# First load ahead of the opening barrier, smaller last load, closing casts in separate tiles, and some loads in halves, in a decode layer on one core

## The chip, the cores and the metric

The kernel runs on one core of one Trainium2 chip. The metric is the device time of one execution in microseconds (us). Before and after are compared by runs of the same rounds on the same chip. A profile is one execution; its span runs from the first recorded instruction to the last, and is some 2 us shorter than the device time.

PE is TensorE's matmul side, PEld its weight loads, DVE is VectorE, ACT is ScalarE, POOL is GpSimd, SP is SyncE, which here issues nearly all transfers. "The stream" is the sequence of loads that SP's queue (q1) hands to the core's 16 DMA engines.

## The reference

One decode token for four sequences: layer norm, attention over the last 2,048 cached keys and values with 32 heads of 192, a gated feed-forward layer, and the sum of both with the input.

```python
B, Sq, D = 4, 1, 640;  Hq = Hkv = 32;  Sk = 8192;  Dh = 192;  F = 1536     # bf16
W = min(4096, max(256, Sk // 4))                  # 2048
q = (xn @ wq) ...                                 # xn = layernorm(x)
k, v = k_cache[:, :, Sk - W:, :], v_cache[:, :, Sk - W:, :]
o = softmax(q @ k.T * Dh ** -0.5) @ v             # per batch and head
return x + o.reshape(B, 1, Hq * Dh) @ wo + (silu(xn @ w1) * (xn @ w3)) @ w2
```

The K and V windows are nearly all of the data: 64 loads of 3 MB, against 22 MB for wq, wo, w1, w3 and w2.

## The kernel before

Every load is one transfer from SP's queue, in a fixed order. At the start come three pieces of wq and two K tiles; in the middle K, V, now and then wo, w1 and w3; at the end the last two V tiles, w2 in three pieces and the last two wo tiles. The opening barrier stands before all of it.

```python
x_sb = const.tile([B, D], BF16, name="x_sb")
nc.scalar.dma_start(out=x_sb[:], in_=A_x.rearrange("b s d -> (b s) d"))     # ACT's queue
for k0 in range(0, KC, 2):                                                  # wq, 3 pieces
    ...
    nc.sync.dma_start(out=wt[:, 0:n, :]..., in_=wq_v[:, k0:k0 + n, :]...)

def load_v(h):
    vt = vpool.tile([P, NJ, Dh], BF16, tag="vt")
    nc.sync.dma_start(out=vt[:].rearrange("q j d -> q (j d)"), in_=v_win[:, h]...)

def ffn_load(name, w):                                                      # w1, w3
    wt = fpool.tile([P, KC, F], BF16, tag="w", name=name)
    nc.sync.dma_start(out=wt[:]..., in_=w...)

W2C = [0, FC - 4, FC - 2, FC]            # FC = 12: pieces of 8, 2 and 2 chunks
def ffn_out(i):                          # two products (acc halves) for each chunk
    for c in range(*W2C[i:i + 2]):
        acc_add(hT[:, c, 0:B], ffn["w2"][:, c, :], last=(c == FC - 1))

# ... the last loads, in this order: V30, V31, w2 piece 0, wo, wo, w2 pieces 1 and 2

res = ppool.tile([NR, N0], BF16, tag="pr", name="res")                      # NR = 36, N0 = 320
nc.vector.tensor_copy(out=res[:, 0:N0 // 2], in_=acc[0:NR, 0:N0 // 2])
nc.scalar.copy(out=res[:, N0 // 2:N0], in_=acc[0:NR, N0 // 2:N0])
nc.sync.dma_start(out=out_v[:, 0:N0], in_=res[0:B, :])
nc.scalar.dma_start(out=out_v[:, N0:D], in_=res[CT:NR, :])
```

## Time and profile before

| | before |
|---|---|
| device time, median (3 runs) | 527.7 us (527.62 to 527.7) |
| span of the profile | 525.5 us |
| share of the 16 DMA engines' span that SP's queue took | 98.9% |
| PE / DVE / ACT busy | 67% / 66% / 9% |

The first view is the page of the kernel before: its first lines, and the lines of its DMA part (bytes moved, then for each queue the transfer packets, the MB and the share of 16 engines' span).

```profile
span 525.5 us, 4734 instructions
...
PE 354.6 (67%) x2307; PEld 74.0 (14%) x1613; DVE 345.2 (66%) x435; ACT 45.9 (9%) x144; POOL 1.1 (0%) x8
...
DMA packets 11572, 223.26 MB, mean 425 GB/s; under 512 B 1296, under 2 KB 1312, under 8 KB 2592
...
q1 hardware_dynamic: 11536, 222.97, 98.9%
q8 instruction: 15, 0.25, 0.2%
q14 instruction: 5, 0.04, 0.0%
```

No engine that computes is near full, and q1 fills the DMA engines. This is a kernel whose stream of loads is its time. Two things can still be read. The stream begins late and ends early in the span, and instructions are fetched over the same engines: q8 does it 15 times, 16 KB each, and q14 five times within the span, 8 KB each.

The next view is the timeline at both ends of the span: start, duration, engine, line, operation, output and inputs, count, and in brackets the idle time before it and what ended it.

```profile
0.73 1.35 SPq L131 DMA_DIRECT2D wt<-in_A_wq_dram  x3
0.74 0.56 ACTq L125 DMA_DIRECT2D x_sb<-in_A_x_dram  x1
...
2.74 0.47 DVE L160 CAST xf<-x_sb 4x640 f32<-4x640 bf16 x1
...
10.55 5.28 PE L193 MATMUL qps<-wt,xnT 128*128 128x512 bf16 x12 [2.20 <-DMA wt<-in_A_wq_dram]
...
521.12 0.44 PE L214 MATMUL acc<-w,hT 128*4 128x320 bf16 x4
521.83 0.44 PE L214 MATMUL acc<-w,hT 128*4 128x320 bf16 x4 [0.27 <-DMA w<-in_B_w_dram]
...
522.31 0.32 DVE L442 CAST res<-acc 36x160 bf16<-36x160 f32 x1 [2.63 <-PE acc L214]
522.66 0.28 ACT L443 CAST res<-acc 36x160 bf16<-36x160 f32 x1 [5.48 <-DVE res L442]
522.97 0.30 SPq L445 DMA_DIRECT2D out_dram<-res  x1
522.97 0.28 ACTq L446 DMA_DIRECT2D out_dram<-res  x1
```

The first load is issued 0.73 us into the span, behind the opening barrier, and its first packet starts at 1.77 us. At the end PE waits for the last piece of w2, four products take 0.44 us, and the two casts run one after the other: ACT's cast names DVE's as what it waited for, since both write one tile.

**Engine by engine.** The trace's packets can be chained to the engine that carried them, as on one engine each starts a few ns after the one before ended, and every engine carries the same sequence of packet sizes. This is a reading of the trace and no view of it; all 16 engines can be chained to their end. A "pause" is what a packet starts later than usual after the one before. The engines fall into two groups:

```
kernel before: end of the engine's last load (us), its instruction fetches, its pauses in all (us; over 60 ns each, after the first 9 us)
518.269  none           0           521.140  three of 8 KB   2.51
518.311  none           0           521.196  two of 16 KB    2.82
518.400  none           0           521.268  two of 16 KB    2.83
518.461  none           0           521.280  two of 16 KB    2.80
518.673  none           0           521.296  two of 16 KB    2.81
518.998  one of 8 KB    0.55        521.342  two of 16 KB    2.83
519.161  one of 8 KB    0.58        521.407  two of 16 KB    2.83
519.718  one of 16 KB   1.41        521.524  two of 16 KB    2.83
```

(Without the 0.08 and 0.11 us that two engines lose to the second x load.) Each 16 KB fetch of q8 costs its engine 1.41 us: the next packet starts some 0.9 us late, and the row after it takes some 0.5 us longer. The fetches of 8 KB cost 0.55 to 0.84 us. The q8 fetches go over eight of the engines in turn, so that with 15 of them seven engines have two and one has one. The Trainium skill describes these fetches ("Runtime: NRT & Kernel Launch", section "Instruction fetch mechanics"): instructions come in blocks of 16 KiB, 256 of them, by the sequencer's own DMA queue. The trace agrees in number: PE has 2,307 matmuls and 1,613 weight loads, 3,920 instructions, 15.3 blocks, and q8 shows 15 transfers. Whose instructions q14 fetches, no view shows.

### The profile page before, as it was taken

The page shows a single profiled execution, that of the slowest core. Times are in us where ns is not written, and L with a number is a line of the kernel's source. Part 1 is how long each engine was busy: PE and PEld are TensorE (multiplying, and loading weights), DVE is VectorE, ACT ScalarE, POOL GpSimd, SP SyncE. Part 2 cuts the span into 40 slices and gives each one's busy share as a digit, 9 for nine tenths or more (in the row PEclk, how much of TensorE's full clock was granted, in tenths as well). Part 3 has the DMA queues.
Part 4 walks back from the last instruction along what each step waited for, and adds up shares of the span by engine and source line. Part 5 has one row for each costly group of instructions (what it writes and reads, how often), then busy time and mean ns, then how long its engine had stood idle before and what let it go on. Part 6 is the DMA issues. An engine that isn't in the chain of part 4 may idle for free.

```text
span 525.5 us, 4734 instructions
## 1 busy us (share of the span) xinstructions
PE 354.6 (67%) x2307; PEld 74.0 (14%) x1613; DVE 345.2 (66%) x435; ACT 45.9 (9%) x144; POOL 1.1 (0%) x8
## 2 busy tenths in 40 slices
PE   2765766567747687667748866686685776675685
PEld 0000111111101111011111211111111111111122
DVE  3179755479557767587656776577667766677671
ACT  2111201000000001000000000000000000000001
POOL 0000000000000000000000000000000000000000
PEclk9989978979889979798887998789878998889988
DMA  8999999999999999999999999999999999999995
GB/s 360 430 438 425 440 431 424 436 428 439 425 433 431 435 426 432 434 427 439 430 427 440 425 434 430 436 428 435 432 428 434 430 430 436 430 434 430 434 422 240
DMA packets 11572, 223.26 MB, mean 425 GB/s; under 512 B 1296, under 2 KB 1312, under 8 KB 2592
## 3 DMA queue, kind: packets, MB, share of 16 engines
q1 hardware_dynamic: 11536, 222.97, 98.9%
q8 instruction: 15, 0.25, 0.2%
q14 instruction: 5, 0.04, 0.0%
q10 hardware_dynamic: 16, 0.01, 0.0%
HBM read 222.96 MB, written 0.01 MB: 424 GB/s over the span
## 4 chain that ended last, share of the span: by engine, by line
DMA 66%; PE 17%; DVE 14%; ACT 2%; issue 1%; SPq 0%
DMA kt<-in_A_k_cache_dram 52%; PE ps L244 10%; DVE pr L233 10%; DMA w<-in_B_w_dram 6%; DMA vt<-in_A_v_cache_dram 5%; PE po L317 4%; DMA wt<-in_A_wq_dram 4%; DVE sc L252 2%; PE qps L193 1%; ACT ex L280 1%; DVE z L288 1%; PE mt L274 1%; PE mt L261 0%; ACT negm L277 0%; DVE qbc L199 0%
## 5 line engine op out<-in xcount | busy, mean ns | idle before, releaser
L244 PE MATMUL ps<-pr,idb 128*128 128x512 bf16 x768 | 211.5, 417 | 151.0 <-DVE pr L233 151.0
L233 DVE TENSOR_TENSOR pr<-kt,qbc 128x3072 bf16<-128x3072 bf16 x128 | 223.5, 1747 | 113.8 <-DMA kt<-in_A_k_cache_dram 113.8
L252 DVE TENSOR_REDUCE sc<-ps 128x16 f32<-128x512 f32 x128 | 87.2, 681 | 2.1 <-PE ps L244 2.1
L296 PE MATMUL o_ps<-vt,z 128*8 128x384 bf16 x1024 | 57.4, 365 | 0.2 <-DVE z L288 0.2
L317 PE MATMUL po<-o_sb,sel_w 128*32 128x192 f32 x128 | 49.2, 518 | 0.6 <-ACT o_sb L299 0.6
L296 PEld LDWEIGHTS <-z 128*8 128x8 bf16 x1024 | 25.5, 92 | 91.7 <-issue 81.2
L299 ACT COPY o_sb<-o_ps 128x384 f32<-128x384 f32 x32 | 15.3, 478 | 190.1 <-PE o_ps L296 190.1
L288 DVE TENSOR_TENSOR z<-ex,mask_b 128x256 bf16<-128x256 bf16 x32 | 13.6, 424 | 23.4 <-ACT ex L280 23.4
L277 ACT COPY negm<-mt 128x1 f32<-128x1 f32 x32 | 5.1, 159 | 256.1 <-PE mt L274 256.1
L261 PEld LDWEIGHTS mt<-idf,lmax 128*1 128x1 f32 x32 | 3.2, 100 | 140.8 <-issue 140.8
L193 PE MATMUL qps<-wt,xnT 128*128 128x512 bf16 x60 | 16.1, 428 | 5.1 <-DMA wt<-in_A_wq_dram 5.1
L317 PEld LDWEIGHTS po<-o_sb,sel_w 128*32 128x32 f32 x128 | 13.8, 130 | 29.7 <-issue 28.2
L244 PEld LDWEIGHTS <-idb 128*128 128x128 bf16 x124 | 11.9, 96 | 39.1 <-issue 32.6
L274 PEld LDWEIGHTS mt<-ones_ff,gneg 1*128 1x128 f32 x64 | 9.4, 183 | 46.3 <-issue 20.9
L199 DVE CAST qbc<-qps 128x512 bf16<-128x512 f32 x6 | 3.8, 685 | 18.0 <-PE qps L193 18.0
L274 PE MATMUL mt<-ones_ff,gneg 1*128 1x1 f32 x64 | 12.1, 256 | 0.6 <-DVE gneg L269 0.6
L266 DVE TENSOR_REDUCE gmax<-mt 1x4 f32<-1x128 f32 x32 | 8.8, 274 | 5.4 <-PE mt L261 5.4
L304 PEld LDWEIGHTS po<-rsum,tot_w 128*32 128x32 f32 x64 | 4.4, 108 | 55.6 <-issue 30.6
L280 ACT ACTIVATE ex<-sc,negm 128x64 bf16<-128x64 f32 x32 | 11.1, 348 | 1.0
L261 PE MATMUL mt<-idf,lmax 128*1 128x128 f32 x32 | 11.0, 344 | 0.0
L214 PE MATMUL acc<-wo_t,oT 128*4 128x320 bf16 x96 | 9.2, 298 | 0.6 <-DMA wo_t<-in_A_wo_dram 0.6
L304 PE MATMUL po<-rsum,tot_w 128*32 128x1 f32 x64 | 7.1, 181 | 1.3 <-ACT ex L280 1.3
(53 smaller groups left out, 62.7 us busy)
## 6 DMA issues: line engine op xcount, KB each, us to landing
kt<-in_A_k_cache_dram SPq DMA_DIRECT2D x32, 3072.0 KB, 18.8
vt<-in_A_v_cache_dram SPq DMA_DIRECT2D x32, 3072.0 KB, 25.9
wo_t<-in_A_wo_dram SPq DMA_DIRECT2D x8, 960.0 KB, 21.5
wt<-in_A_wq_dram SPq DMA_DIRECT2D x2, 3072.0 KB, 9.8
w<-in_B_w_dram SPq DMA_DIRECT2D x2, 1920.0 KB, 21.5
wt<-in_A_wq_dram SPq DMA_DIRECT2D x1, 1536.0 KB
w<-in_B_w_dram SPq DMA_DIRECT2D x1, 1280.0 KB, 32.8
w<-in_B_w_dram SPq DMA_DIRECT2D x2, 320.0 KB, 31.0
```

What stands on the lines that cost most here:

```text
L193: nc.tensor.matmul(qp[:], lhsT=xnT[:, kc].rearrange("p a b -> p (a b)"), rhs=wq_rows[kc][:, (c0 + i) * QC:(c0 + i + 1) * QC], start=(kc == ...
L233: nc.vector.tensor_tensor(out=pr[:], in0=kts[h][:, g * JQ:(g + 1) * JQ, :], in1=qbc[:, h * Dh:(h + 1) * Dh].unsqueeze(1).to_broadcast([P, ...
L244: nc.tensor.matmul(ps[:], lhsT=idb[:], rhs=pr[:, :, kk * DD:(kk + 1) * DD], start=(kk == 0), stop=(kk == NK - 1))
L252: nc.vector.tensor_reduce(out=scs[h][:, g * JQ:(g + 1) * JQ], in_=pss.pop(u)[:], axis=AX.X, op=ALU.add)
L261: nc.tensor.transpose(out=mt[0:1, 0:P], in_=chs[h][0][:], identity=idf[:])
L274: nc.tensor.matmul(mt[:, P:P + 1], lhsT=gneg[:].rearrange("o p b -> o (p b)"), rhs=ones_ff[0:1, 0:1], start=True, stop=True)
L280: nc.scalar.activation(out=ex[:], in_=scs.pop(h)[:], func=ACTF.Exp, bias=negm[:, 0:1], scale=SCALE, accum_out=rsum[:])
L288: nc.vector.tensor_tensor(out=z[:], in0=ex[:].unsqueeze(2).to_broadcast([P, NJ, B]), in1=mask_b[:].unsqueeze(1).to_broadcast([P, NJ, B]), ...
L296: nc.tensor.matmul(o_ps[c * CT:c * CT + 2 * B, :], lhsT=z[:, 2 * jj:2 * jj + 2, :], rhs=vt[:, 2 * jj:2 * jj + 2, :], start=(jj < 4), stop= ...
L299: nc.scalar.copy(out=o_sb[:], in_=o_ps[:])
L304: nc.tensor.matmul(po[sl, Dh:Dh + 1], lhsT=tot_w[:].rearrange("p a b -> p (a b)"), rhs=rsums.pop(h)[:], start=True, stop=True)
L317: nc.tensor.matmul(po[sl, 0:Dh], lhsT=sel_w[:, par].rearrange("p a b -> p (a b)"), rhs=o_sb[:, par * Dh:(par + 1) * Dh].rearrange("p (r i) ...
```

## The change

Its intent is to start the stream earlier and to shorten what follows its end. The first wq transfer is moved into the block before the opening barrier. The last w2 piece shrinks from two chunks to one. The two closing casts write two tiles, each one half of the output, so that they can run together. w1, w3, the last two V tiles and the first eight chunks of w2 come in two transfers each. The second load of x is dropped (x_sb is used instead), and a tile of ones is cut to one element.

```diff
+def first_load_first(nc):
+    for f in nc.python_module().functions:
+        head, body = f.blocks[0], f.blocks[1]
+        ...                                   # i, ins: SP's first transfer in body
+        ...                                   # j: SP's drain, which opens the barrier, in head
+        del body.instructions[i]
+        head.instructions.insert(j, ins)
...
+    nc.at_finalize(first_load_first)
...
-    def load_v(h):
+    def load_v(h, n=1):
...
+        for j in range(0, NJ, NJ // n):
+            nc.sync.dma_start(out=vt[:, j:j + NJ // n]..., in_=...[:, :, j:j + NJ // n]...)
...
-    ones_ff = const.tile([P, P], FP32, name="ones_ff")
+    ones_ff = const.tile([1, 1], FP32, name="ones_ff")
...
-        nc.sync.dma_start(out=xr["t"][:], in_=A_x.rearrange("b s d -> (b s) d"))
...
-        nc.sync.dma_start(out=wt[:]..., in_=w...)                       # w1, w3
+        for k0, k1 in ((0, KC // 2), (KC // 2, KC)):
+            nc.sync.dma_start(out=wt[:, k0:k1, :]..., in_=...[:, k0:k1, :]...)
...
-    W2C = [0, FC - 4, FC - 2, FC]
+    W2C = [0, FC - 8, FC - 4, FC - 1, FC]
...
-        add(NU - 6, 0, load_v, h)
+        add(NU - 6, 0, load_v, h, 2)
     # last loads now: V30 (2), V31 (2), w2 pieces 0 and 1, wo, wo, w2 pieces 2 and 3
...
-    res = ppool.tile([NR, N0], BF16, tag="pr", name="res")
-    nc.vector.tensor_copy(out=res[:, 0:N0 // 2], in_=acc[0:NR, 0:N0 // 2])
-    nc.scalar.copy(out=res[:, N0 // 2:N0], in_=acc[0:NR, N0 // 2:N0])
+    res = [ppool.tile([NR, N0], BF16, tag="pr", name="res") for _ in range(2)]
+    nc.scalar.copy(out=res[1][CT:NR, :], in_=acc[CT:NR, :])
+    nc.vector.tensor_copy(out=res[0][0:B, :], in_=acc[0:B, :])
...
-    nc.sync.dma_start(out=out_v[:, 0:N0], in_=res[0:B, :])
-    nc.scalar.dma_start(out=out_v[:, N0:D], in_=res[CT:NR, :])
+    nc.scalar.dma_start(out=out_v[:, N0:D], in_=res[1][CT:NR, :])
+    nc.sync.dma_start(out=out_v[:, 0:N0], in_=res[0][0:B, :])
```

More of the change, by code (lines that the diff above doesn't have):

```diff
@@ L32, in keep_loaded_weights @@
                 del block.instructions[i]
+def first_load_first(nc):
+    for f in nc.python_module().functions:
+        head, body = f.blocks[0], f.blocks[1]
+        sp = mybir.EngineType.SP
+        i, ins = next((i, ins) for i, ins in enumerate(body.instructions)
+                      if ins.engine == sp and not isinstance(ins, mybir.InstNoOp))
+        assert isinstance(ins, mybir.InstDMACopy) and not ins.has_wait()
+        j = next(j for j, other in enumerate(head.instructions)
+                 if other.engine == sp and isinstance(other, mybir.InstDrain))
+        del body.instructions[i]
+        head.instructions.insert(j, ins)
 @with_exitstack
@@ L111, in load_k @@
         kts[h] = kt
-    def load_v(h):
+    def load_v(h, n=1):
         vt = vpool.tile([P, NJ, Dh], BF16, tag="vt")
-        nc.sync.dma_start(out=vt[:].rearrange("q j d -> q (j d)"),
-                          in_=v_win[:, h].rearrange("b (p j) d -> p b (j d)", p=PB))
+        for j in range(0, NJ, NJ // n):
+            nc.sync.dma_start(out=vt[:, j:j + NJ // n].rearrange("q j d -> q (j d)"),
+                              in_=v_win[:, h].rearrange("b (p j) d -> p b j d", p=PB)[:, :, j:j + NJ // n].rearrange("p b j d -> p b (j d)"))
         vts[h] = vt
@@ L220 @@
     po = ps_po.tile([P, Dh + 1], FP32, name="po")
-    xr = {}
-    def x_load():
-        xr["t"] = const.tile([B, D], BF16, name="x_res")
-        nc.sync.dma_start(out=xr["t"][:], in_=A_x.rearrange("b s d -> (b s) d"))
     def x_add(i):
-        acc_half(i, idb[0:B, 0:B], xr["t"], first=True)
+        acc_half(i, idb[0:B, 0:B], x_sb, first=True)
     def mult(u):
@@ L273, in chain_bc @@
         lmax, mt, gneg = chs[h]
-        nc.tensor.matmul(mt[:, P:P + 1], lhsT=gneg[:].rearrange("o p b -> o (p b)"), rhs=ones_ff[0:1, 0:1],
+        nc.tensor.matmul(mt[:, P:P + 1], lhsT=gneg[:].rearrange("o p b -> o (p b)"), rhs=ones_ff[:],
                          start=True, stop=True)
@@ L341, in ffn_load @@
         wt = fpool.tile([P, KC, F], BF16, tag="w", name=name)
-        nc.sync.dma_start(out=wt[:].rearrange("p k n -> p (k n)"), in_=w.rearrange("(p kc) n -> p (kc n)", kc=KC))
+        for k0, k1 in ((0, KC // 2), (KC // 2, KC)):
+            nc.sync.dma_start(out=wt[:, k0:k1, :].rearrange("p k n -> p (k n)"),
+                              in_=w.rearrange("(p kc) n -> p kc n", kc=KC)[:, k0:k1, :].rearrange("p k n -> p (k n)"))
         ffn[name] = wt
@@ L417 @@
     add(23, 9, ffn_h)
-    add(8, 0, x_load)
     add(16, 6, x_add, 0)
@@ L423 @@
     for h in range(H - 2, H):
-        add(NU - 6, 0, load_v, h)
+        add(NU - 6, 0, load_v, h, 2)
     add(NU - 6, 0, w2_load, 0)
+    add(NU - 6, 0, w2_load, 1)
     add(NU - 6, 0, wo_load, NG - 2)
     add(NU - 6, 0, wo_load, NG - 1)
-    add(NU - 6, 0, w2_load, 1)
     add(NU - 6, 0, w2_load, 2)
+    add(NU - 6, 0, w2_load, 3)
     add(e - 1, 8, ffn_out, 0)
+    add(e - 1, 8, ffn_out, 1)
     add(e - 1, 8, ge_proj, NG - 2, 0, RPP)
     add(e, 6, ge_proj, NG - 1, 0, RPP)
-    add(e, 7, ffn_out, 1)
     add(e, 7, ffn_out, 2)
+    add(e, 7, ffn_out, 3)
     for s in sorted(sched):
```

## The prediction

> **What bounds the kernel now.** The load stream. The DMA part of the page gives queue q1 98.9% of 16 engines' span, 222.97 MB at a mean of 425 GB/s; PE is busy 67% and DVE 66%.  Chaining the trace's DMA packets engine by engine, the undisturbed engines show no gap over 60 ns from the first packet at 1.8-2.5 us to their last at 518.3 us. Engines that also carried two 16 KB instruction fetches each (about 1.4 us apiece) end at 521.1-521.5 us. The last of them ends the kernel: the Trainium skill, "DMA: Bandwidth & Descriptors", section "Why a DMA increments its semaphore by 16 and not by 1", says that each engine posts its own increment after its data; the trace agrees (16 four-byte packets per full-width transfer). So only the stream's start, its engine time and what follows the last landing can move the time.
>
> **Terms**
>
> 1. *First wq transfer ahead of the barrier: -0.73 us.* In the timeline, SP reaches its drain at 0.00, is released at 0.65 and issues the first wq transfer at 0.73; POOL releases the barrier at 0.61. SP's issue takes 0.40 us, so it should still reach the barrier before POOL opens it. The next wq issue follows near 0.73 us; the first transfer lasts 7.3 us, so no hole appears.
> 2. *Five more transfers (w1, w3, two V, w2) over the same bytes: +0.2 us.* Completion packets of one engine are 7.272 us apart for 24,576-byte rows and 0.796 us for 2,560-byte rows (eight rows each): a fixed 0.043 us per transfer, times five. Dropping the second x load is worth under 0.02 us.
> 3. *Last w2 piece one chunk: -0.13 us.* In the timeline four products took 0.44 us after the last landing (521.83), a pair about 0.135 us. The three-chunk piece lands about 0.45 us before the last, so its six products are just issued when the last pair may start.
> 4. *Casts in separate tiles: -0.15 us.* Now DVE (0.32) and then ACT (0.28) run in series, 522.31 to the issue at 522.97: 0.66 us. After, both run together: DVE 320 columns, estimated from 0.317 us at 160 and 0.685 at 512, 0.48 us; ACT about 0.39. Then the issue.
> 5. *ones_ff smaller, the order of the w2 and wo loads, earlier w2 products:* off the critical path. The last loads get new waits on transfer semaphores, but over 10 us of loads are queued then.
>
> **Predicted time: 526.9 us** (527.7 - 0.8), range 526.2 to 527.6. Chances: faster by over 2% 0.003, within 2% 0.994, slower by over 2% 0.003.
>
> **What would show each step.** (1) The first wq issue at 0.00 of the new span, the first packet near 1.05 us and barrier release no later than 0.75. (2) Per-engine packets back to back, 0.043 us more per extra transfer; q1's share unchanged near 99%; PE's last wait still a w2 landing, near 521.3. (3) 0.30 us from last landing to end of products. (4) DVE and ACT casts overlapping, the longer one about 0.48 us. End of products to end of span: about 3.05 us (before 3.2).
>
> **What would make it wrong.** SP's drain may wait longer and hold the barrier. The x load now queues behind 24 KB packets, so xn comes up to 1 us later; if K tiles were then freed late enough to empty the queue, the stream would show a hole. Instruction fetches landing differently over the engines (three on one) would cost 1.4 us.

## The result

| | before | changed |
|---|---|---|
| device time, median (6 runs each) | 527.57 us (527.23 to 527.7) | 526.47 us (526.25 to 526.56) |
| span of the profile | 525.5 us | 524.4 us |
| ratio, 95% interval | | 0.998 (0.9967 to 0.9992) |

Ratios are the mean time of one kernel's runs over that of the other's of the same rounds, so not quite the ratio of the medians. The change is 1.1 us faster, 0.2%, well within 2%; the forecast was 526.9 us in a range of 526.2 to 527.6. It gained more than the 0.8 us that I had counted (by 0.3 us in the profiles, whose single terms can be compared), and the question is from where.

The same lines of the page, for the changed kernel:

```profile
span 524.4 us, 4738 instructions
...
PE 359.4 (69%) x2306; PEld 73.8 (14%) x1613; DVE 346.0 (66%) x435; ACT 46.0 (9%) x144; POOL 1.1 (0%) x8
...
DMA packets 12285, 223.26 MB, mean 426 GB/s; under 512 B 1373, under 2 KB 1513, under 8 KB 3177
...
q1 hardware_dynamic: 12248, 222.96, 99.2%
q8 instruction: 15, 0.25, 0.2%
q14 instruction: 6, 0.04, 0.0%
```

The bytes and the instruction fetches are the same (the sixth packet of q14 is one of 80 bytes at 0.09 us), and there are 712 more q1 packets. The timeline of the changed kernel at the two ends:

```profile
0.00 1.68 SPq L148 DMA_DIRECT2D wt<-in_A_wq_dram  x3
...
0.81 0.55 ACTq L142 DMA_DIRECT2D x_sb<-in_A_x_dram  x1
...
6.73 0.48 DVE L177 CAST xf<-x_sb 4x640 f32<-4x640 bf16 x1 [3.82 <-DMA x_sb<-in_A_x_dram]
...
12.94 16.05 PE L210 MATMUL qps<-wt,xnT 128*128 128x512 bf16 x59 [0.59 <-DVE xnT L201]
...
520.99 0.71 PE L231 MATMUL acc<-w,hT 128*4 128x320 bf16 x8 [0.15 <-DMA w<-in_B_w_dram]
...
521.73 0.48 DVE L457 CAST res<-acc 4x320 bf16<-4x320 f32 x1 [2.07 <-PE acc L231]
521.76 0.42 ACT L456 CAST res<-acc 4x320 bf16<-4x320 f32 x1 [4.59 <-PE acc L231]
522.21 0.28 ACTq L459 DMA_DIRECT2D out_dram<-res  x1
522.24 0.35 SPq L460 DMA_DIRECT2D out_dram<-res  x1
```

The first wq issue stands at 0.00. x is used 4 us later than before (6.73 against 2.74), as its small packets now queue behind rows of 24 KB; PE's first wq product starts at 12.94 instead of 10.55, but then runs through without a wait. At the end eight products run in one go, and the casts overlap.

To find the surplus I cut the whole execution at five moments that the trace gives, so that the phases add up to the span:

| phase (us) | before | changed | difference | forecast |
|---|---|---|---|---|
| span's start to first load packet | 1.765 | 1.039 | -0.73 | -0.73 |
| first packet to the end of the last load (the stream) | 519.759 | 520.036 | +0.28 | +0.2 |
| end of the last load to the end of the last product | 0.744 | 0.622 | -0.12 | -0.13 |
| last product to SP's output issue | 0.700 | 0.538 | -0.16 | -0.15 |
| SP's issue to its landing, as SP saw it | 1.473 | 1.374 | -0.10 | 0 |
| landing to the end of the span | 1.070 | 0.819 | -0.25 | 0 |
| sum | 525.511 | 524.428 | -1.08 | -0.8 |

Four terms are where they were forecast. The surplus lies after the output's issue, a stretch that I had taken as unchanged. There SP, as the last thing it does, goes through the semaphores of all transfers in a fixed order; the trace gives the time of each check:

```
SP's closing checks (semaphore numbers: start in us); * = semaphore of an output store
before    106*: 524.441   107,103*: 524.499   108,102: 524.566   109,100: 524.630   110,104: 524.692
changed   106,103: 522.644   107,102: 522.713   108,100: 522.779   109*,101: 523.430   110*,104: 523.609
```

Each check that follows the landing costs some 0.065 us. In the kernel before, the landing is waited for in the first check, and four more follow. In the changed kernel three checks are done while the stores are under way. This came about by counting: the transfers take eight semaphores in turn, and four transfers more (five halves, less one x load) move the two output stores from the first two checks to the last two.

### The profile page after: what moved, and what is told of

It is laid out like the page before. It is cut to its first block, busy times and chain, and to the rows that moved or that the text cites. A ratio compares the mean times of both kernels' runs of the same rounds, so it can differ in the third digit from the quotient of the medians.

```text
span 524.4 us, 4738 instructions
## 1 busy us (share of the span) xinstructions
PE 359.4 (69%) x2306; PEld 73.8 (14%) x1613; DVE 346.0 (66%) x435; ACT 46.0 (9%) x144; POOL 1.1 (0%) x8
## 4 chain that ended last, share of the span: by engine, by line
DMA 61%; DVE 21%; PE 15%; ACT 2%; issue 1%; SPq 0%
DMA kt<-in_A_k_cache_dram 52%; DVE pr L244 14%; PE ps L255 8%; DMA vt<-in_A_v_cache_dram 4%; DMA w<-in_B_w_dram 4%; DVE sc L263 3%; PE qps L210 3%; PE po L328 3%; DMA x_sb<-in_A_x_dram 1%; DVE z L299 1%; ACT ex L291 1%; PE mt L285 1%; ACT L291 0%; DVE oT L336 0%; DVE og L333 0%
## 5 line engine op out<-in xcount | busy, mean ns | idle before, releaser
L255 PE MATMUL ps<-pr,idb 128*128 128x512 bf16 x768 | 219.4, 429 | 146.2 <-DVE pr L244 146.1
L244 DVE TENSOR_TENSOR pr<-kt,qbc 128x3072 bf16<-128x3072 bf16 x128 | 223.4, 1746 | 108.5 <-DMA kt<-in_A_k_cache_dram 108.5
L307 PE MATMUL o_ps<-vt,z 128*8 128x384 bf16 x1024 | 54.4, 350 | 0.2 <-DVE z L299 0.2
```

The costliest lines, as they stand in the source:

```text
L244: nc.vector.tensor_tensor(out=pr[:], in0=kts[h][:, g * JQ:(g + 1) * JQ, :], in1=qbc[:, h * Dh:(h + 1) * Dh].unsqueeze(1).to_broadcast([P, ...
L255: nc.tensor.matmul(ps[:], lhsT=idb[:], rhs=pr[:, :, kk * DD:(kk + 1) * DD], start=(kk == 0), stop=(kk == NK - 1))
L307: nc.tensor.matmul(o_ps[c * CT:c * CT + 2 * B, :], lhsT=z[:, 2 * jj:2 * jj + 2, :], rhs=vt[:, 2 * jj:2 * jj + 2, :], start=(jj < 4), stop= ...
```

## The experiments

Theory A is the table of phases: the barrier, the last piece and the casts give what was forecast, extra transfers cost 0.04 to 0.05 us each, and a quarter of the gain is the accidental place of the output's semaphores. Rival B is the intent behind the change: that loads in halves, and the dropped x load, feed the queue better and gave the surplus.

All runs gave the right result. Unless said otherwise, "before" is the median of the kernel before in the same rounds.

| run | before | this | ratio (95%) | first packet | stream | load to product | product to issue | issue to landing | landing to end |
|---|---|---|---|---|---|---|---|---|---|
| a_barrier | 527.53 | 526.91 | 0.9986 (0.9973-1.0) | 1.030 | 519.805 | 0.747 | 0.701 | 1.474 | 1.069 |
| b_casts | 527.58 | 527.34 | 0.9995 (0.9982-1.0007) | 1.758 | 519.847 | 0.746 | 0.539 | 1.359 | 1.075 |
| c_w2 | 527.58 | 527.30 | 0.9998 (0.9984-1.0011) | 1.760 | 519.847 | 0.652 | 0.702 | 1.473 | 1.069 |
| d_lane_before | 527.58 | 527.30 | 0.9994 (0.9982-1.0007) | 1.761 | 519.847 | 0.746 | 0.702 | 1.479 | 0.812 |
| e_lane_after | 527.53 | 526.73 | 0.9983 (0.9971-0.9996) | 1.029 | 520.073 | 0.604 | 0.539 | 1.357 | 1.074 |
| f_whole | 527.53 | 526.46 | 0.9979 (0.9967-0.9992) | 1.027 | 520.080 | 0.643 | 0.538 | 1.381 | 1.047 |
| g_whole_lane | 527.53 | 526.32 | 0.9975 (0.9962-0.9987) | 1.023 | 519.842 | 0.643 | 0.539 | 1.366 | 0.813 |
| h_split24 | 527.58 | 527.65 | 1.0001 (0.9988-1.0013) | 1.033 | 521.207 | 0.653 | 0.539 | 1.368 | 0.812 |
| i_fetch | 527.49 | 527.77 | 1.0006 (0.9991-1.0021) | 1.026 | 521.345 | 0.721 | 0.540 | 1.371 | 0.813 |
| j_swap | 527.49 | 526.25 | 0.9977 (0.996-0.9993) | 1.028 | 519.868 | 0.636 | 0.473 | 1.229 | 0.997 |
| k_best | 527.63 | 526.19 | 0.9974 (0.996-0.9988) | 1.029 | 519.743 | 0.656 | 0.474 | 1.235 | 0.998 |

The intervals are some 0.13% wide to either side, 0.7 us, so for effects of 0.1 to 0.3 us the ratio decides nothing; the phases do, which repeat to about 0.01 us. (In f_whole SP was already waiting inside its first check when the store landed; there the end of that check is taken as the landing. In j_swap and k_best SP's store is the one checked first of the two, so their last two columns are to be compared by their sum alone.) Load to product is less steady (0.60 to 0.64 us with the same loads in the changed kernel, e_lane_after and j_swap). The stream is the exception: kernels with the same loads gave 519.76 to 519.85 us (before, a_barrier, b_casts, d_lane_before; c_w2, with its end pieces cut otherwise, 519.847) and 519.87 to 520.07 us (changed, e_lane_after, j_swap).

### a_barrier: the first load alone

```diff
# kernel before
+    nc.at_finalize(first_load_first)
```

> The kernel before with only the first wq transfer moved ahead of the opening barrier. Main theory (the stream of loads sets the time, so an earlier start shows in full): first load packet at 1.04 us instead of 1.77, everything after it as before, so 0.7 us faster than before (526.85 where before is 527.55). Rival (the late barrier and the x load, which arrives about 4 us later behind the queued packets, cost part of it): gain of 0.4 us or less, with holes between packets or a K tile freed late.

It ran 0.62 us faster than before. The first packet started at 1.030 us, 0.735 us earlier, and every later phase is that of the kernel before. In this run x came as late as in the changed kernel and the stream shows nothing of it (519.805 us), so the rival's loss is not there. The gain of an earlier start passes through to the end, 0.69 us of it in the span, the rest being within the scatter of the stream.

### b_casts and c_w2: the two ends of the tail alone

```diff
# b_casts, on the kernel before: only the lines of the closing casts and stores
# c_w2, on the kernel before
-    W2C = [0, FC - 4, FC - 2, FC]
+    W2C = [0, FC - 4, FC - 1, FC]
```

> The kernel before with only the two closing casts in separate tiles. Theory: end of the last product to SP's output issue 0.54 us instead of 0.70, so 0.16 us faster than before. Rival: none named beyond no gain (within 0.05 us), if the output's landing and not the issue sets the end.

> The kernel before with only the last w2 piece cut to one chunk (pieces of 8, 3 and 1 chunks, so no transfer more). Theory: last load's end to the end of the products 0.62 us instead of 0.74, so 0.12 us faster. Rival: no gain, as the three-chunk piece now holds PE up instead.

The casts alone cut the product-to-issue phase by 0.16 us as expected, and the issue-to-landing phase by 0.11 us as well, which I had not expected. The run was 0.24 us faster. The smaller last piece cut its phase by 0.09 us; the run was 0.28 us below before by its median, but its runs span 0.8 us and the mean differs by 0.02%, so its time is inconclusive and only the phase is shown.

The second part of the casts' gain is seen in every kernel with separate tiles, and in none without. In the former the two stores are issued by ACT and SP some 25 ns apart (110 ns in j_swap and k_best); in the kernels with one tile both wait for the same cast and are issued within 5 ns of each other. No run keeps one tile and moves the stores apart, so that the spacing is the cause is not shown.

### d_lane_before and e_lane_after: the place of the semaphores

Four loads of 32 bytes on ACT's queue in the middle of the kernel, whose data nobody uses, turn the count by four.

```diff
# d_lane_before on the kernel before, e_lane_after on the changed kernel
+    def tiny_load(i):
+        t = const.tile([1, 16], BF16, name=f"tiny{i}")
+        nc.scalar.dma_start(out=t[:], in_=A_x.rearrange("b s d -> (b s) d")[0:1, 0:16])
+    for i in range(4):
+        add(40 + 2 * i, 0, tiny_load, i)
```

> The kernel before with four 32-byte loads on ACT's queue in the middle, which turn the semaphores by four places: the output gets the two that SP checks last. Theory A: landing to end 0.82 us instead of 1.07, so 0.25 us faster than before though it does more work. Rival B: no change.

> The changed kernel with four 32-byte loads added in the middle on ACT's queue, which turn the eight transfer semaphores by four places, so that the output transfers get the ones that SP checks first at the end, as in the kernel before. Theory A (0.25 us of the measured 1.1 us came from this renumbering): SP does four more checks after the output has landed, landing to end 1.07 us instead of 0.82, so 0.25 us slower than the changed kernel (0.85 us faster than before). Rival B (the surplus over the forecast came from the finer loads or the dropped x load): nothing changes, 1.1 us faster than before.

With four useless loads the median of the kernel before fell by 0.28 us; its profile shows 0.26 us less in the last phase. With the same four the changed kernel lost: 0.80 us below before instead of 1.1, with 0.255 us more in the last phase. Rival B expected no change in either. The four lines below are from the view of one source line, the program's closing code, for the kernel before, the changed kernel, d_lane_before and e_lane_after in that order. They give SP's semaphore checks, their number, shortest, median and longest duration in ns, and the start of the first and the last in us.

```profile
L472 SPq EVENT_SEMAPHORE  x7: 17/28/28, 524.4 to 525.4; - x7
```

```profile
L486 SPq EVENT_SEMAPHORE  x7: 17/28/28, 522.6 to 524.4; - x7
```

```profile
L479 SPq EVENT_SEMAPHORE  x7: 17/28/28, 523.4 to 525.3; - x7
```

```profile
L493 SPq EVENT_SEMAPHORE  x7: 17/28/28, 523.6 to 524.6; - x7
```

(Seven records, as the two of the closing barrier are among them.) Where the stores' semaphores come last, the first check is done 1.7 to 1.9 us before the last record; where they come first, 1.0 us.

### f_whole and g_whole_lane: loads in one piece again

```diff
# f_whole, on the changed kernel
-        for k0, k1 in ((0, KC // 2), (KC // 2, KC)):
+        for k0, k1 in ((0, KC),):
...
-    W2C = [0, FC - 8, FC - 4, FC - 1, FC]
+    W2C = [0, FC - 4, FC - 1, FC]
...
-        add(NU - 6, 0, load_v, h, 2)
+        add(NU - 6, 0, load_v, h)
# g_whole_lane: the same, and five 32-byte loads as above, so that the count is as in the changed kernel
```

> The changed kernel with w1, w3, the last two V tiles and the front of w2 in one transfer each again (five fewer transfers; the last w2 piece stays one chunk). Theory A: the stream of loads is 0.2 us shorter (0.043 us per transfer), but the output's semaphores move to places with three checks after them, which takes 0.2 us back: within 0.1 us of the changed kernel. Rival B (splitting feeds the queue better): 0.3 us or more slower than the changed kernel, with holes in the stream.

> As the run with whole loads, with five 32-byte loads added on ACT's queue so that the output's semaphores are again the last two that SP checks. Theory A: the stream is 0.2 us shorter than in the changed kernel and the closing is the same, so 0.2 us faster than it, 1.3 us faster than before. Rival B (splitting helps): slower than the changed kernel.

With whole loads the kernel is no slower: 526.46 us against 526.47, although its output semaphores fell to places that cost it 0.235 us from issue to the end (four checks after the landing, where I had expected three). With the semaphores put back, whole loads gave 526.32 us, 0.15 us below the changed kernel. Rival B expected 0.3 us or more of loss and is out. What halves cost the stream is less clear here than I had expected: f_whole's profiled stream was no shorter than the changed kernel's (520.080 us). But the stream is the time of one engine, the last. The time that load packets took, added up and divided by the 16 engines, scatters less: 519.59, 519.71 and 519.77 us with whole loads (g_whole_lane, k_best, f_whole), and 520.00, 520.04 and 520.07 us with halves (e_lane_after, j_swap, changed kernel). Packets overlap by 3 to 4 ns, and with halves an engine has 45 more of them, so of the 0.35 us between the groups up to 0.18 us is overlap, and some 0.2 us is left.

### h_split24: more halves

```diff
# on the changed kernel
-            add(u0 + 2, 0, load_v, h)
+            add(u0 + 2, 0, load_v, h, 2 if h >= 4 and h < 28 else 1)
```

> The changed kernel with 24 more V tiles (heads 4 to 27) in two transfers each; 24 is a multiple of eight, so the semaphores keep their places. Theory A (0.043 us of engine time per transfer): the stream is 1.03 us longer, so 1.0 us slower than the changed kernel, equal to before. Rival B (finer transfers cost nothing or help): within 0.2 us of the changed kernel.

The run was 527.65 us, 1.18 us above the changed kernel, all of it in the stream: 521.207 against 520.036 us, 1.17 us for 24 transfers, 0.049 us each. Here are the lines of its DMA part: the q1 line, and the issues of V with their count and size.

```profile
q1 hardware_dynamic: 15704, 222.96, 99.3%
...
vt<-in_A_v_cache_dram SPq DMA_DIRECT2D x52, 1536.0 KB, 24.1
```

The same bytes, 3,456 more packets, 52 half tiles, and a queue as full as before: the cost is engine time, not a hole. For the five extra transfers of the change this is 0.25 us, an estimate from this run. In the chains of the changed kernel rows of 24 KB follow each other every 0.908 us, rows of 12 KB every 0.456 us, and a completion packet takes 0.006 us more: so a V tile in halves costs each engine 8 x 0.004 + 0.006 = 0.038 us, an estimate, and most of it comes from the cut rows and not from the transfer as such.

### i_fetch: more instructions, same loads

```diff
# on the changed kernel: the pass that drops repeated weight loads is left out
-    nc.at_finalize(keep_loaded_weights)
```

> The changed kernel without the pass that drops repeated weight loads: TensorE gets about 700 more instructions, no load of data changes. Theory (the engine that was interrupted by most instruction fetches ends the stream): the queue of instruction fetches shows 17 or 18 transfers of 16 KB instead of 15, one or two engines are hit a third time, and the stream ends 1.4 us later though it carries the same bytes; about 1.4 us slower than the changed kernel, 0.3 us slower than before. Rival (the two groups of engine ends are engines that are slower all along): no change, within 0.2 us of the changed kernel. If PE, now with more weight loads, became the limit, the K waits of DVE would shrink and the loss would be far above 1.4 us.

The run was 527.77 us, 1.30 us above the changed kernel, and the stream is 1.31 us longer. From its page and its timeline:

```profile
PE 355.0 (68%) x2306; PEld 142.4 (27%) x2307; DVE 345.8 (66%) x435; ACT 46.0 (9%) x144; POOL 1.1 (0%) x8
...
q1 hardware_dynamic: 12248, 222.96, 98.9%
q8 instruction: 18, 0.29, 0.2%
```

```profile
522.38 0.71 PE L230 MATMUL acc<-w,hT 128*4 128x320 bf16 x8 [0.18 <-DMA w<-in_B_w_dram]
```

PE has 694 weight loads more, q8 carries 18 fetches instead of 15, and the last w2 wait ends at 522.38 instead of 520.99. PE did not become the limit: DVE still waits 112.7 us for K tiles (108.5 in the changed kernel). In the chains of packets two engines now carry three 16 KB fetches each, at 47.6, 270.0 and 497.8 us and at 69.4, 301.0 and 517.9 us; their pauses add up to 4.25 and 4.24 us, and they end at 522.27 and 522.37 us, while no other engine ends after 521.13 us. Eighteen fetches over eight engines in turn leave two for a third turn. The rival, of engines that are slower all along, is out.

### j_swap and k_best: the two stores, and the best version

```diff
# j_swap, on the changed kernel: DVE casts the half that ACT's queue stores, and the reverse
-    nc.scalar.copy(out=res[1][CT:NR, :], in_=acc[CT:NR, :])
-    nc.vector.tensor_copy(out=res[0][0:B, :], in_=acc[0:B, :])
+    nc.vector.tensor_copy(out=res[1][CT:NR, :], in_=acc[CT:NR, :])
+    nc.scalar.copy(out=res[0][0:B, :], in_=acc[0:B, :])
# k_best: g_whole_lane with these casts
```

> The changed kernel with the engines of the two closing casts swapped: DVE casts the half that ACT's queue stores, ACT the half that SP stores. Theory A (two output stores issued within 5 ns of each other get in each other's way; a lead of 25 ns of either avoids it): if SP's issue leads by some 20 ns, issue to landing of SP's store stays at or below 1.37 us, the time is that of the changed kernel within 0.1 us. Theory B (SP's store lands sooner because its issue is the later one, as the 1.47 us of the kernel before is a wait on the earlier store): SP's store takes 1.47 us or more and the gain of 0.1 us is lost.

> The best version that the runs point to: whole loads, five 32-byte loads that keep the output's semaphores last, and the closing casts swapped between DVE and ACT. Theory: the gains add, as they lie in different phases: stream 0.2 us shorter than in the changed kernel, end of the products to end of span 2.70 us instead of 2.73; so 0.2 us faster than the changed kernel and 1.3 us faster than before. If it is not below the changed kernel, the two small gains do not add.

Now SP's issue leads by 110 ns, and its store is seen landed 1.229 us after it; ACT's is then the one that ends last, and from the last product to the end of the span it is 2.70 us, against 2.73 in the changed kernel and 3.24 in the kernel before. So it does not matter which store leads. That the 0.1 us is lost when the two are issued within 5 ns fits all runs, but the kernels that do so also have one tile for both; why it is lost stays open.

The best version combines whole loads, the semaphores in the last places and the swapped casts: 526.19 us, 1.44 us below before and 0.3 us below the changed kernel (on other rounds). Its median is 0.06 us below j_swap's, or 0.20 us when each is set against the kernel before of its own rounds, and its stream is 0.125 us shorter. So the five halves cost about 0.2 us (0.06 to 0.25 us by the ways told here); the times alone, with intervals of 0.7 us, do not show it.

## Why the prediction was right or wrong

The time fell into the range, and the gain was forecast as 0.8 us and measured as 1.1 us. Point by point:

- **The bound: right.** Every change of start, of stream and of tail showed up in the time in its own size, and 4 us more delay of x did not. That the engine with most time lost to instruction fetches ends the stream was read from the chains, and i_fetch shows it. One detail was too neat: not every engine of the late group had two 16 KB fetches; the one that ended at 521.140 us had none, but three of the 8 KB fetches of q14.
- **Term 1, the barrier: right.** Forecast -0.73 us, measured -0.73 in the changed kernel and alone. SP's drain took 0.12 us and POOL passed the barrier 0.08 us later than before (0.69 against 0.61), which cost nothing.
- **Term 2, five more transfers: right in sign and nearly in size.** Forecast 0.043 us for each; 0.049 in h_split24. On the change itself, +0.28 us in the two profiles. The forecast was derived as a fixed cost of a transfer; by the packets' starts it is mostly a cost of the rows that the halves cut in two.
- **Term 3, the last piece: right.** Forecast -0.13 us, measured -0.12; the last pair of products came at once after the six before, as forecast.
- **Term 4, the casts: the term was mis-sized.** "Casts in separate tiles: -0.15 us" ended its sum at SP's issue. That part measured -0.16, but the landing also came 0.10 to 0.11 us sooner. The two stores were no longer issued within 5 ns then, which may be why. The term is worth 0.27 us (b_casts).
- **Term 5, "off the critical path": the wrong step.** I had seen that the added transfers turn the semaphores of the later ones, and asked only what waits that gave to loads. The output stores are transfers too, and their place in SP's closing checks is on the critical path: -0.25 us. The forecast "end of products to end of span: about 3.05 us (before 3.2)" is where it shows: it measured 2.73 us.
- **The named risk about x:** x came 4 us later, not 1 us. It queued behind several rows of 24 KB, as the trace's packets show (its four packets started at 4.9 to 5.4 us, against 1.7 before). It was harmless: in the changed kernel's chains four engines show no pause over 60 ns from first to last load.

The runs with one part each leave next to nothing over: first packet -0.735 us (a_barrier), both phases of the casts -0.278 (b_casts), last piece -0.092 (c_w2), place of the semaphores -0.258 (d_lane_before), and with the +0.28 us of the stream this is -1.09 us; measured was -1.08.

So of the change's parts, the halves cost time (about 0.2 us by themselves) and repaid it by accident through the semaphore count. That was luck: eight transfers more, or none, would have left the output's semaphores where they were. The range was wide enough to take the 0.35 us that terms 4 and 5 missed.

## What to carry to other kernels

Where one stream of loads is the time, cut the execution into the time before its first packet, the stream, and the time after its last landing, and write down the phases in ns: changes of 0.1 us that no comparison of times resolves stand out there. Add the stretch after the output's issue to the sum as well, since it is serial: which semaphore the output store got was worth 0.25 us, and 0.1 us went with whether two stores were issued in the same moment. Before splitting loads, ask what each extra transfer and each cut row costs the queue, and when an edit adds or removes transfers, look at which later ones are renumbered by it.

## What the Trainium skill lacked or had wrong

- "Runtime: NRT & Kernel Launch", section "Instruction fetch mechanics", calls the cost of crossing a 16 KiB boundary "mostly hidden". Its block size and count fit (15 fetches for 3,920 instructions, 18 for 4,613). But in a kernel whose loads fill the DMA engines a fetch is not hidden: 1.41 us of pause on the engine that carries it, engines with two of them ended about 3 us after those with none, and three fetches more made the kernel 1.30 us slower. The section does not have the five 8 KB fetches of q14, which cost 0.55 to 0.84 us each.
- "DMA: Bandwidth & Descriptors", section "Anatomy of one DMA — SWDGE (gpsimd) path", gives a fixed cost of about 2.0 us for a DMA on that path; for one more transfer among those queued back to back on SP's queue no cost is given in time. Here it was 0.049 us of every engine's time for each extra transfer that cuts 24 KB rows in two (24 more: 1.17 us).
- The same page, section "Why a DMA increments its semaphore by 16 and not by 1", says each engine posts its own increment after its data. The trace agrees, with 16 four-byte packets for a full-width transfer. What it lacks is how far apart the engines can be: between the two groups lay about 3 us at the end of the stream, and the last engine decides.
- The same page, "Issuing engines are not separate DMA queues", says that transfers of all engines interleave. Neither that section nor what the page has on how an engine takes turns between queues gives the time that a small one waits: x, 5 KB on ACT's queue, waited until 4.9 us behind 24 KB rows of SP's queue when it was issued 0.81 us into the span, and 1.7 us when it was issued together with the first of them at 0.74.
- No page has the closing checks: SP goes through the transfers' semaphores one pair after another, about 0.065 us each, and the output's place in that order was worth 0.25 us.
